# The last two rows of w2 in a decode block: two one-row transfers, the last of them cut into 112, 8 and 8 partitions

## The chip, the cores and the metric

The kernel runs on one core of a Trainium2 chip. The metric is the device time of one execution in microseconds (us), as the median over runs. A profile is one execution of the same program with the hardware profiler on; its span is the time from the first to the last instruction that the profile shows, and its own time is a little longer than that. Times in a profile are counted from the start of the span.

## The reference

One decode step (one token for each of four sequences) of a transformer block: layer norm, attention with grouped heads over the last 2048 entries of a cache, a residual, layer norm, a gated feed-forward part, a residual. All weights are bf16.

```python
def _B_ref(x, w1, w3, w2):            # x: [4, 1, 1024]
    gate = x @ w1                     # w1, w3: [1024, 3584]
    up = x @ w3
    h = silu(gate) * up
    return h @ w2                     # w2: [3584, 1024]

h  = x + A_ref(layernorm(x), k_cache, v_cache, wq, wo)
h2 = h + B_ref(layernorm(h), w1, w3, w2)
```

There are only four tokens, so each weight is read once and used for little arithmetic: 55.58 MB come from memory for about 1.7 thousand small matmuls and weight loads.

## The kernel before

All large inputs (wq, the k and v caches, wo, w1, w3, w2) go through one list, `jobs` (lines 80 to 98). Each job is one transfer of up to 2 MB into a slot of 16 KB for each of 128 partitions; there are ten slots (`NSLOT`, line 18), used in turn. `load_up_to` (line 102) issues jobs in the list's order from SyncE's queue, and `get` (line 115) is called where a job's data are first used: it issues everything up to ten jobs ahead and hands back the view of the slot. Which instruction waits for which is worked out by the tile framework, from the slots and from the semaphores of the transfers: there are eight of these, used in turn by the transfers of SyncE and ScalarE, so a transfer also waits for the one eight places ahead of it.

The order is wq (4 jobs), k (4), v (4), wo (4), w1 (4), w3 (4), w2 (5). In w2, partition p holds the 28 rows from 28p on, of 1024 numbers (2 KB) each. `W2B` (line 94) cuts these 28 rows into jobs of 8, 8, 8, 2 and 2 rows, so the last job brings two rows for each partition, 4 KB in one piece, 512 KB in all.

The product with w2 is at the end of the kernel (lines 365 to 379). For each of a job's rows there are four matmuls (line 371), one for each quarter of the 1024 outputs; they go to four column groups of TensorE and add up in one tile, `y2_ps`, over all 28 rows. The weights that each matmul loads first are the 32 columns of `hg_T` for that row, not w2; w2 is the moving operand. Since a matmul reads all 128 partitions of its row, it needs the whole of that row's transfer. After the last of the 112 matmuls VectorE adds the residual (`res`, line 381), and four stores of 2 KB, two from SyncE and two from ScalarE, write the result (line 384).

Of the kernel before, what the change touches and what calls it, by code (L numbers as in the profile page):

```python
# [10 lines left out]
P = 128  # L11
# [11 lines left out]
def kernel(  # L23
# [19 lines left out]
    nc = tc.nc  # L43
# [36 lines left out]
    jobs = []  # L80
    for i in range(KC // 2):
        jobs.append(("wq", i, [2, NQ], wq_v[:, 2 * i : 2 * i + 2, :]))
    for g in range(Hkv):
        src = A_k_cache[:, g, Sk - W : Sk, :].rearrange("b (p j) d -> p b j d", j=NK)
        jobs.append(("k", g, [B, NK, Dh], src))
    for b in range(B):
        src = A_v_cache[b, :, Sk - W : Sk, :].rearrange("g (p j) d -> p g j d", j=NK)
# [3 lines left out]
    for name, w_v in (("w1", w1_v), ("w3", w3_v)):  # L91
        for i in range(KC // 2):
            jobs.append((name, i, [2, F], w_v[:, 2 * i : 2 * i + 2, :]))
    W2B = [8, 8, 8, 2, 2]
    f0 = 0
    for i, n in enumerate(W2B):
        jobs.append(("w2", i, [n, D], w2_v[:, f0 : f0 + n, :]))
        f0 += n
    place = {(name, i): at for at, (name, i, _, _) in enumerate(jobs)}
    loaded = []  # L100

    def load_up_to(at):
        while len(loaded) < min(at, len(jobs)):
            name, i, shape, src = jobs[len(loaded)]
            slot = stream.tile([P, SLOT], BF16, tag="slot", name="s_" + name)
            n = int(np.prod(shape))
            view = slot[:, :n]
            if len(shape) == 2:
                view = view.rearrange("p (a b) -> p a b", a=shape[0])
            else:  # L110
                view = view.rearrange("p (a b c) -> p a b c", a=shape[0], b=shape[1])
            nc.sync.dma_start(out=view, in_=src)  # L112
            loaded.append(view)

    def get(name, i):
        at = place[(name, i)]
        load_up_to(at + NSLOT)
        return loaded[at]
# [4 lines left out]
    for c in range(C):  # L123
        nc.scalar.dma_start(out=x_nat[R * c : R * c + B, :], in_=x_flat[:, c * DQ : (c + 1) * DQ])
    load_up_to(NSLOT)

    ident = const.tile([P, P], BF16)
# [7 lines left out]
        out=gmask[:, :, 0],  # L135
        in_=ident[:].rearrange("p (b g r) -> p g b r", b=B, g=Hkv),
# [73 lines left out]
    for b in range(B):  # L210
        nc.vector.tensor_copy(
            out=Qm[:, b].rearrange("p (g y) -> p g y", y=QW)[:, :, :REP],
            in_=qT_ps[:, :, :, b].rearrange("p r g -> p g r"),
# [19 lines left out]
    for g in range(Hkv):  # L233
        k = get("k", g)
        for nb in range(NK // JB):
            kT = ktpool.tile([P, B, JB, P], BF16, tag="kT")
            for bb in range(2):
                kt_ps = ps.tile([P, 2, JB, P], BF16, tag=f"kt{n_step % 4}")
                for b2 in range(2):
                    for jj in range(JB):  # L240
                        nc.tensor.transpose(  # L241
                            out=kt_ps[:, b2, jj],
                            in_=k[:, 2 * bb + b2, nb * JB + jj, :],
# [20 lines left out]
        out=Pm[:], in_=sc_ps[:], func=ACT.Exp, bias=nmax[:], scale=qscale, accum_out=rsum[:]  # L264
# [4 lines left out]
    for jb in range(NK // 8):  # L269
        pt_ps = ps.tile([P, 8, P], BF16, tag=f"kt{jb}")  # L270
        for jj in range(8):
            j = jb * 8 + jj
            nc.tensor.transpose(  # L273
                out=pt_ps[:, jj], in_=Pm[:, j * P : (j + 1) * P], identity=ident[:]
# [9 lines left out]
    for j in range(NK):  # L284
# [11 lines left out]
        out=o_sb[:],  # L296
# [69 lines left out]
    fc = 0  # L366
    for i, n in enumerate(W2B):
        w = get("w2", i)
# [46 lines left out]
```

## Time and profile before

| | us |
|---|---|
| median of 3 runs | 141.52 (141.49 to 141.57) |
| the profiled execution | 141.43 |
| its span | 139.4 |
| last transfer of w2 issued, landed | 105.72, 135.45 |
| addition of the residual (line 381) starts | 136.16 |
| first store issued | 136.61 |

How to read it: the chain of waits is followed back from the last instruction, at each step to what released it; 77% of the span lies there in transfers and 16% in TensorE. In the timeline a row gives start, length, engine, line, operation and the number of instructions merged, with the idle time before them in brackets and what ended it. In windows each engine has its busy time and count in a stretch, and the last three numbers are TensorE's granted clock (1.0 is full speed), the mean busy share of the 16 DMA engines, and GB/s. PEld is the loading of weights into TensorE. The trace also holds a record of each DMA packet (start, duration, size and queue, but not which of the 16 engines it ran on) and of each time that a transfer's semaphore rises (its landings, one for each engine that took part).

### The profile page before, as it was taken

The numbers are of one execution on the slowest core, as the hardware profiler recorded it, in microseconds if no ns is written. First come the engines' busy times: TensorE is split into PE (matmuls) and PEld (weight loads), VectorE is DVE, ScalarE is ACT, GpSimd is POOL, SyncE is SP. The second block draws the span as 40 slices with busy tenths as digits, with TensorE's granted clock in tenths as the row PEclk, the third lists the DMA queues.
The fourth block names the chain that finished last, engine by engine and source line by source line (L and its number), as shares of the span: only waits on it lengthen the run. The fifth ranks groups of instructions, "written<-read, shape, count | busy, mean of one in ns | idle before, by whom it ended". The sixth has DMA issues, their size and how long they took to land.

```text
span 139.4 us, 1934 instructions
## 1 busy us (share of the span) xinstructions
PE 69.0 (49%) x848; PEld 42.3 (30%) x848; DVE 32.5 (23%) x58; ACT 26.2 (19%) x27; POOL 2.7 (2%) x10
## 2 busy tenths in 40 slices
PE   0015535499898898039844225272340093352370
PEld 0012111297666574036433213130110041041250
DVE  0023000332443334601110002400019900610001
ACT  1100000135575755266000000310020000000000
POOL 7000000000000000000000000000000000000000
PEclk9999985556999999755896555555555559555555
DMA  5999999999999999999999999999999999999940
GB/s 150 444 414 423 451 437 381 411 425 411 422 424 409 427 420 415 424 413 410 408 404 405 410 441 431 432 424 436 424 432 432 432 432 435 418 437 437 400 197 2
DMA packets 10903, 55.70 MB, mean 400 GB/s; under 512 B 496, under 2 KB 528, under 8 KB 8976
## 3 DMA queue, kind: packets, MB, share of 16 engines
q1 hardware_dynamic: 10848, 55.58, 96.4%
q8 instruction: 6, 0.10, 0.2%
q10 hardware_dynamic: 48, 0.01, 0.0%
q14 instruction: 1, 0.01, 0.0%
HBM read 55.58 MB, written 0.01 MB: 399 GB/s over the span
## 4 chain that ended last, share of the span: by engine, by line
DMA 77%; PE 16%; ACT 2%; SPq 2%; issue 1%; DVE 0%; ACTq 0%
DMA s_w<-in_B_w_dram 41%; DMA s_wo<-in_A_wo_dram 17%; DMA s_k<-in_A_k_cache_dram 14%; PE kt_ps L241 11%; DMA s_wq<-in_A_wq_dram 5%; PE sc_ps L224 3%; ACT kT L249 2%; SPq L112 2%; PE y_ps L319 1%; PE y_ps L371 0%; DVE res L381 0%; ACTq L249 0%
## 5 line engine op out<-in xcount | busy, mean ns | idle before, releaser
L342 PE MATMUL gu_ps<-s_w,n_T 128*32 128x448 bf16 x128 | 12.3, 544 | 18.9 <-DVE eg L357 8.7
L241 PE MATMUL kt_ps<-ident,s_k 128*128 128x128 bf16 x256 | 18.8, 237 | 1.1 <-DMA s_k<-in_A_k_cache_dram 1.1
L249 ACT COPY kT<-kt_ps 128x1024 bf16<-128x1024 bf16 x16 | 15.9, 1013 | 13.4 <-PE kt_ps L241 13.4
L241 PEld LDWEIGHTS <-s_k 128*128 128x128 bf16 x256 | 16.6, 107 | 4.0 <-issue 2.7
L247 DVE COPY kT<-kt_ps 128x1024 bf16<-128x1024 bf16 x16 | 11.1, 692 | 16.2 <-PE kt_ps L241 16.2
L342 PEld LDWEIGHTS <-n_T 128*32 128x32 bf16 x128 | 4.9, 130 | 25.7 <-issue 20.1
L371 PE MATMUL y_ps<-s_w,hg_T 128*32 128x256 bf16 x112 | 6.7, 415 | 9.6 <-DMA s_w<-in_B_w_dram 9.5
L319 PE MATMUL y_ps<-s_wo,oT 128*32 128x256 bf16 x128 | 6.5, 368 | 9.2 <-DMA s_wo<-in_A_wo_dram 8.8
L192 PE MATMUL q_ps<-s_wq,n_T 128*32 128x512 bf16 x64 | 6.6, 567 | 7.6 <-DMA s_wq<-in_A_wq_dram 5.8
L224 PE MATMUL sc_ps<-kT,Qm 128*32 128x512 bf16 x64 | 9.1, 401 | 1.7 <-ACT kT L249 1.4
L371 PEld LDWEIGHTS <-hg_T 128*32 128x32 bf16 x112 | 4.7, 138 | 12.0 <-issue 7.5
L319 PEld LDWEIGHTS <-oT 128*32 128x32 bf16 x128 | 4.7, 124 | 10.7 <-issue 9.6
L147 PE MATMUL sums_ps<-both,ones_f 128*128 128x64 f32 x4 | 1.3, 440 | 11.5 <-DVE both L145 11.5
L157 ACT ACTIVATE rstd<-rstd,eps_t 128x4 f32<-128x4 f32 x2 | 0.6, 297 | 30.7 <-DVE rstd L156 30.7
L286 PE MATMUL o_ps<-s_v,PT 128*32 128x512 bf16 x64 | 5.8, 529 | 0.0
L356 DVE RECIPROCAL eg<-eg 128x896 f32<-128x896 f32 x1 | 5.8, 5753 | 0.0
L192 PEld LDWEIGHTS <-n_T 128*32 128x32 bf16 x64 | 2.4, 126 | 11.0 <-issue 10.7
L273 PE MATMUL pt_ps<-ident,Pm 128*128 128x128 bf16 x16 | 1.9, 312 | 6.0 <-ACT Pm L263 6.0
L147 PEld LDWEIGHTS sums_ps<-both,ones_f 128*128 128x128 f32 x4 | 1.0, 310 | 11.9 <-DVE both L145 9.7
L224 PEld LDWEIGHTS <-Qm 128*32 128x32 bf16 x64 | 2.3, 93 | 6.2 <-issue 5.1
L328 DVE TENSOR_TENSOR h<-y_ps,x_nat 128x256 f32<-128x256 f32 x1 | 0.4, 425 | 15.3 <-PE y_ps L319 15.3
L286 PEld LDWEIGHTS <-PT 128*32 128x32 bf16 x64 | 3.3, 126 | 2.3 <-issue 1.7
(51 smaller groups left out, 32.7 us busy)
## 6 DMA issues: line engine op xcount, KB each, us to landing
s_w<-in_B_w_dram SPq DMA_DIRECT2D x8, 1792.0 KB, 22.2
s_wq<-in_A_wq_dram SPq DMA_DIRECT2D x4, 2048.0 KB, 13.8
s_k<-in_A_k_cache_dram SPq DMA_DIRECT2D x4, 2048.0 KB, 19.5
s_v<-in_A_v_cache_dram SPq DMA_DIRECT2D x4, 2048.0 KB, 23.0
s_wo<-in_A_wo_dram SPq DMA_DIRECT2D x4, 2048.0 KB, 23.3
s_w<-in_B_w_dram SPq DMA_DIRECT2D x3, 2048.0 KB, 35.6
s_w<-in_B_w_dram SPq DMA_DIRECT2D x2, 512.0 KB, 31.3
x_nat<-in_A_x_dram ACTq DMA_DIRECT2D x4, 2.0 KB
```

Of the source, the lines that this page charges most:

```text
L112: nc.sync.dma_start(out=view, in_=src)
L147: nc.tensor.matmul(sums_ps[:], lhsT=ones_f[:], rhs=both[:], start=True, stop=True)
L192: nc.tensor.matmul(q_ps[R * c : R * c + R, hf * HALF : (hf + 1) * HALF, :], lhsT=xn_T[:, kc, :], rhs=w[:, kk, o : o + HALF * Dh], start=(k ...
L224: nc.tensor.matmul(sc_ps[R * b : R * b + R, nb * 512 : (nb + 1) * 512], lhsT=Qm[:, b, g * R : (g + 1) * R], rhs=kT[:, b], start=(g == 0), ...
L241: nc.tensor.transpose(out=kt_ps[:, b2, jj], in_=k[:, 2 * bb + b2, nb * JB + jj, :], identity=ident[:],)
L247: nc.vector.tensor_copy(out=kT[:, 2 * bb : 2 * bb + 2], in_=kt_ps[:])
L249: nc.scalar.copy(out=kT[:, 2 * bb : 2 * bb + 2], in_=kt_ps[:])
L286: nc.tensor.matmul(o_ps[R * b : R * b + R], lhsT=PT[:, j, R * b : R * b + R], rhs=vs[b][:, :, j, :], start=(j == 0), stop=(j == NK - 1), t ...
L319: nc.tensor.matmul(y_ps[R * c : R * c + R, :], lhsT=oT[:, h, :], rhs=w[:, hh, c * DQ : (c + 1) * DQ], start=(h == 0), stop=(h == Hq - 1), ...
L342: nc.tensor.matmul(out_ps[R * c : R * c + R, hf, :FH], lhsT=hn_T[:, kc, :], rhs=w[:, kk, o : o + FH], start=(kc == 0), stop=(kc == KC - 1) ...
L356: nc.vector.reciprocal(out=eg[:], in_=eg[:])
L371: nc.tensor.matmul(y2_ps[R * c : R * c + R, :], lhsT=hg_T[:, fc, :], rhs=w[:, ff, c * DQ : (c + 1) * DQ], start=(fc == 0), stop=(fc == FC ...
```

## The change

`W2B` gets one job more: the last two rows come in two jobs of one row each (2 KB for each partition, 256 KB). The very last job of the list is issued as three transfers, for partitions 0 to 111, 112 to 119 and 120 to 127, all into the same slot. The four matmuls of the last row then need all three. Nothing else is different; the matmuls are the same 112 in the same order.

```diff
-    W2B = [8, 8, 8, 2, 2]
+    W2B = [8, 8, 8, 2, 1, 1]
...
+    def at_end(name, i):
+        return (name, i) == jobs[-1][:2]
...
-            nc.sync.dma_start(out=view, in_=src)
+            if at_end(name, i):
+                for lo, hi in ((0, P - 16), (P - 16, P - 8), (P - 8, P)):
+                    nc.sync.dma_start(out=view[lo:hi], in_=src[lo:hi])
+            else:
+                nc.sync.dma_start(out=view, in_=src)
             loaded.append(view)
```

Line 371, the matmul with w2, becomes line 378; the loads of line 112 become lines 117 and 119.

## The prediction

> **What bounds the kernel now.** I read the page's busy slices first, then the chain of waits, then the end of the timeline, and last short windows of the tail.
>
> ```profile
> PE 69.0 (49%) x848; PEld 42.3 (30%) x848; DVE 32.5 (23%) x58; ACT 26.2 (19%) x27; POOL 2.7 (2%) x10
> DMA  5999999999999999999999999999999999999940
> GB/s 150 444 414 423 451 437 381 411 425 411 422 424 409 427 420 415 424 413 410 408 404 405 410 441 431 432 424 436 424 432 432 432 432 435 418 437 437 400 197 2
> q8 instruction: 6, 0.10, 0.2%
> ```
>
> No engine is busy half the time, and the DMA row stands at 9 from the second slice to the last but two. The kernel is a stream of 55.58 MB at its full rate. What can be changed is what follows the stream, and how evenly its 16 engines finish. The chain of waits shows the end:
>
> ```profile
> 105.72 29.73 DMA s_w<-in_B_w_dram
> 135.45 0.04 issue
> 135.49 0.64 PE y_ps L371 x7
> 136.14 0.02 issue
> 136.16 0.43 DVE res L381
> ```
>
> The last transfer of w2 (two rows of 2 KB for each partition) was issued at 105.72 and landed at 135.45, nearly 30 us later: it lay in the queue behind the others. Then come its eight matmuls, the addition and the stores. Two rows of the timeline and three windows (time, length, engines, granted clock, DMA share, GB/s) show that TensorE is done with all else before then, and how the stream ends:
>
> ```profile
> 133.08 3.04 PE L371 MATMUL y_ps<-s_w,hg_T 128*32 128x256 bf16 x48 [2.96 <-DMA s_w<-in_B_w_dram]
> 135.50 0.14 PEld L371 LDWEIGHTS <-hg_T 128*32 128x32 bf16 x7 [0.40 <-issue]
> 133.50:134.00 0.50, 0.50 (x16) 0.43 (x12) 0.00 (x0) 0.00 (x0) 0.00 (x0) 0.50 0.53 213
> 134.00:134.50 0.50, 0.50 (x16) 0.42 (x12) 0.00 (x0) 0.00 (x0) 0.00 (x0) 0.50 0.42 172
> 134.50:135.00 0.50, 0.50 (x20) 0.41 (x9) 0.00 (x0) 0.00 (x0) 0.00 (x0) 0.50 0.34 139
> ```
>
> From 133.5 on the DMA share is half, then a third. The trace's landing records of the last transfer, one for each engine, say why: nine engines land from 133.70 to 134.12, one at 134.78, six from 135.22 to 135.45 (the slowest three 135.38, 135.41, 135.45). The first transfer landed within 0.45 us (7.57 to 8.02). The six 16 KB packets of the instruction queue (31.2, 43.0, 53.5, 70.4, 91.6, 122.1) each put one more engine about 1.4 us behind; an 8 KB one at 74.4 made the seventh. Every transfer is cut evenly over 16 engines, so this lateness is kept to the end.
>
> **The change, part by part.** The sum is made against the profiled execution: 141.43 us, of which 139.4 are span and 2.0 lie around it. It is 0.09 below the median of the runs shown, 141.52.
>
> (a) *Fewer matmuls after the last landing: four, where there were eight.* In the trace's rows the first four start at 135.49 to 135.50 and take up to 0.40, ending at 135.90; the other four end at 136.11. So 0.21 leaves the path. The same pitch stands in the 48 above: twelve groups of four in 3.04 us, less a gap of 0.3 and the last one's 0.42, are 0.21 each. The four of the row before come when its bytes land, about half a small transfer (0.6 us) earlier, and take that 0.21 while the last row is on its way; without this cover the gain would be gone.
>
> (b) *The wait moves from a matmul to a weight load.* Built, the changed kernel's first weight load of the last row waits for both 8-partition transfers and its matmul for the 112-partition one. Before, the matmul alone waited, with weights loaded ahead. Behind the waiting load stand only this row's seven other instructions and, after them, VectorE's addition. The trace has both kinds for line 342: at 90.33 the load waited and its matmul started 2 ns later, taking 553 ns; at 111.79 the matmul waited and took 532. That is 0.02 and touches only the first of four. A second semaphore may need an instruction of its own: those on TensorE took 0.05, and the next load came 0.08 after its start. Bounds 0.00 and 0.10. I take 0.05, as one of the two waits will usually be over early.
>
> (c) *2 KB pieces in place of 4 KB.* Windows in the stages with 4 KB, 2 KB and 16 KB or 14 KB pieces:
>
> ```profile
> 48.00:60.00 12.00, 6.79 (x88) 4.36 (x83) 5.25 (x7) 6.50 (x7) 0.00 (x0) 0.89 1.02 420
> 64.00:80.00 16.00, 9.16 (x149) 5.92 (x145) 1.04 (x2) 1.85 (x2) 0.00 (x0) 0.71 1.05 407
> 125.00:132.00 7.00, 2.05 (x36) 1.39 (x32) 0.00 (x0) 0.00 (x0) 0.00 (x0) 0.50 1.01 431
> ```
>
> The packet records agree: on one engine a 4 KB packet follows the last after 155.6 ns, a 2 KB one after 80.0. Eight pairs are 8 x (160.0 - 155.6) = 0.035 us more. A further transfer adds one semaphore packet (about 5 ns); three add at most 0.02. I take 0.04 (bounds 0.035 and 0.06).
>
> (d) *The split.* 112 partitions are seven pieces on each of 16 engines. How an 8-partition load is laid out, no row shows; the nearest is the 4-partition load of x, whose semaphore rose once at issue and then four times, one piece on each of four engines. So an 8-partition transfer should take eight engines with one piece each. If both take the same eight, these carry nine pieces in all and the other eight seven, where all had eight: +0.08 for the one half, -0.08 for the other. If they take different halves, 0. The end is set by the slowest of the six late engines, so bounds are -0.08 and +0.08. Were the late engines spread at random over the two halves, the very latest would be in the loaded half one time in two. I take +0.08.
> [...]
>
> (e) *Issue.* SyncE issues three transfers more at 0.33 each (its rows for w2 near the end). It waits for the transfer eight places ahead on its semaphore, so the last small one goes out once w3's last part has landed, at about 118.4. Its turn in the queue comes at about 134, so 15 us hide it. The tenth-last slot, w1's last part, is read long before (by about 102). Only the stores are queued behind on SyncE, and they wait for 136.6. Cost 0; were the cover gone, the stream would stand still for what is late.
>
> Sum: -0.21 + 0.05 + 0.04 + 0.08 = -0.04. The bounds are -0.21 + 0.00 + 0.035 - 0.08 = -0.26 and -0.21 + 0.10 + 0.06 + 0.08 = +0.03. On the profiled execution 141.39, on the median 141.48.
>
> **The rivals.**
>
> *The late engines lie in the spared half.* Then (d) is -0.08, and with a free wait the median comes to 141.26, with (b) as taken 141.32. For it: nothing shows which engines were late. Against it: all of the three latest, which are within 0.07 us, must be in that half, about one time in eight. By itself this stays just within 0.2% (0.28 us, about the least that a measurement of this kernel tells from no change); with 0.03 more from elsewhere it is over.
>
> *The small transfers end one after the other, slower.* If a transfer of eight pieces does not flow behind the one ahead but pays its own way from start to completion, the last landing is late by that. Nearest row: a store of 2 KB at the end is issued at 136.61 and its last landing is recorded at 138.04, so 1.43. One such at the end gives 141.52 + 1.43 - 0.21 + 0.05 + 0.04 = 142.8. It decides from 0.45 us on, where the gain of (a) is eaten and 0.28 passed. Against it: the large transfers follow one another without a gap, 8 x 0.607 = 4.86 for w2's, and their landings are 4.86 apart; the queue is filled 15 us ahead.
> [...]
>
> *The small transfer lies on one engine.* Eight pieces on one are 0.64, two transfers 1.28, less the one piece spared. On one of the nine early engines (at most 134.12) that ends at 135.3 and nothing is seen; on a late one it ends 1.2 later, at about 142.6. The four landings of x speak against it.
>
> *The change does nothing*: if its waits cost all that (a) gains, 141.5, which is inside the forecast.
>
> **How the numbers follow.** Forecast with its own bounds (141.26 to 141.55): 0.75. Late engines spared, and a little more: 0.12. Serial ends: 0.08. One engine: 0.05, half of it unseen. Hence faster by over 0.2%: 0.12. Slower: 0.08 + 0.025, with some for a fetch that falls on an engine already late: 0.12. The rest, 0.76, is within. The range takes the forecast's bounds, and on both sides 0.05 to 0.1 for the spread of the runs (0.08): 141.20 to 141.65; what lies above is left out with about 0.12.
>
> **What would show it.** In the chain, four matmuls instead of eight (0.43 to 0.50 after the landing, not 0.68). In the landing records, the last of the 112-partition transfer and of both small ones, 135.4 to 135.6, and eight landings for each small one. A load of line 378 that starts within 0.1 of the last landing. It is wrong if the last landing comes after 135.8, if the stores' issue moves by more than 0.28, or if a gap opens in the DMA row before 133.5.

## The result, and the profile after

The changed kernel takes 141.88 us (median of 8 runs, 141.67 to 142.06) against 141.52 (8 runs, 141.33 to 141.57): a ratio of 1.0025, 95% interval 1.0016 to 1.0033. It is slower by a quarter of a per cent, outside the range that was forecast. The profiled execution took 141.69, with a span of 139.7. The medians and ratios below leave out one execution that was over 1.5% above the fastest of its kernel, the profiled one of the extra loads into spread partitions.

The end of the chain of waits of the changed kernel (start, length, what):

```profile
105.83 29.86 DMA s_w<-in_B_w_dram
135.70 0.04 issue
135.74 0.80 PE y_ps L378 x7
136.54 0.02 issue
136.56 0.42 DVE res L388
```

The addition starts at 136.56, before the change at 136.16. The chain names the landing of the last row but one (135.70); by the landing records the 112-partition transfer of the last row ends at 136.07, and its four matmuls start 0.04 later. Before, the last landing was at 135.45. So the loss is all ahead of the last landing: that is 0.62 later, while the time from there to the addition fell from 0.71 to 0.49.

Windows of the tail of the changed kernel (time, length, engines with busy time and count, granted clock, DMA share, GB/s):

```profile
133.00:133.50 0.50, 0.25 (x8) 0.21 (x11) 0.00 (x0) 0.00 (x0) 0.00 (x0) 0.50 1.03 406
133.50:134.00 0.50, 0.50 (x16) 0.43 (x12) 0.00 (x0) 0.00 (x0) 0.00 (x0) 0.50 0.74 246
134.00:134.50 0.50, 0.50 (x17) 0.40 (x12) 0.00 (x0) 0.00 (x0) 0.00 (x0) 0.50 0.46 127
134.50:135.00 0.50, 0.50 (x19) 0.32 (x9) 0.00 (x0) 0.00 (x0) 0.00 (x0) 0.50 0.45 172
135.00:135.50 0.50, 0.50 (x12) 0.28 (x8) 0.00 (x0) 0.00 (x0) 0.00 (x0) 0.50 0.28 107
```

Divide GB/s by DMA share, which gives the rate that the busy engines would have if all 16 were busy: 394 and 382 in the first and fourth rows, 332 in the second, 276 in the third. Before the change the rows from 133.5 to 135.0 gave 402, 410 and 409. For about 0.9 us the DMA engines are busy and move less. The packet records show the same piece by piece:

```
packets of queue 1, start in us from the span's start, duration in ns
                       before            after
4 KB, 133.0 to 133.5   159 each          159 each
4 KB, 133.6 to 134.1   159 each          159 to 296, eight of eleven over 159
2 KB, 133.8 to 134.3   (none)            107 to 206, but for one of 84
2 KB, from 134.5       (none)            84, a few to 92
all packets            1 slow after 118  30 slow after 118, 2.2 us in all
```

(Slow means more than 8 ns above the usual duration of its size. One slow packet of 16 KB near 123.1, by 0.5 us, is in both kernels.) The slow 4 KB packets are a clue. They belong to the transfer of rows 24 and 25, which the change does not touch, and by their times they are on the engines that run late: the early ones had landed that transfer by 133.03. They turn slow from 133.57 on, as the early engines come to the pieces of the cut (nine had landed the row before it from 133.29 to 133.75).

### The profile page after: what moved, and what is told of

Same layout as the page of the kernel before. It is cut to its first block, busy times and chain, and to the rows that moved or that the text cites. A ratio compares the mean times of both kernels' runs of the same rounds, so it can differ in the third digit from the quotient of the medians.

```text
span 139.7 us, 1939 instructions
## 1 busy us (share of the span) xinstructions
PE 69.5 (50%) x848; PEld 42.8 (31%) x848; DVE 32.5 (23%) x58; ACT 26.2 (19%) x27; POOL 2.7 (2%) x10
## 4 chain that ended last, share of the span: by engine, by line
DMA 77%; PE 15%; ACT 2%; SPq 2%; issue 1%; DVE 0%; ACTq 0%
DMA s_w<-in_B_w_dram 41%; DMA s_wo<-in_A_wo_dram 17%; DMA s_k<-in_A_k_cache_dram 14%; PE kt_ps L248 11%; DMA s_wq<-in_A_wq_dram 5%; PE sc_ps L231 3%; ACT kT L256 2%; SPq L119 2%; PE y_ps L326 1%; PE y_ps L378 1%; DVE res L388 0%; ACTq L256 0%
## 5 line engine op out<-in xcount | busy, mean ns | idle before, releaser
L326 PE MATMUL y_ps<-s_wo,oT 128*32 128x256 bf16 x128 | 5.9, 345 | 9.7 <-DMA s_wo<-in_A_wo_dram 9.3
L199 PE MATMUL q_ps<-s_wq,n_T 128*32 128x512 bf16 x64 | 7.4, 628 | 6.6 <-DMA s_wq<-in_A_wq_dram 4.8
L378 PEld LDWEIGHTS <-hg_T 128*32 128x32 bf16 x112 | 4.8, 135 | 12.4 <-issue 7.9
L293 PEld LDWEIGHTS <-PT 128*32 128x32 bf16 x64 | 3.9, 127 | 1.7 <-DVE PT L284 0.2
```

The costliest lines, as they stand in the source:

```text
L199: nc.tensor.matmul(q_ps[R * c : R * c + R, hf * HALF : (hf + 1) * HALF, :], lhsT=xn_T[:, kc, :], rhs=w[:, kk, o : o + HALF * Dh], start=(k ...
L293: nc.tensor.matmul(o_ps[R * b : R * b + R], lhsT=PT[:, j, R * b : R * b + R], rhs=vs[b][:, :, j, :], start=(j == 0), stop=(j == NK - 1), t ...
L326: nc.tensor.matmul(y_ps[R * c : R * c + R, :], lhsT=oT[:, h, :], rhs=w[:, hh, c * DQ : (c + 1) * DQ], start=(h == 0), stop=(h == Hq - 1), ...
L378: nc.tensor.matmul(y2_ps[R * c : R * c + R, :], lhsT=hg_T[:, fc, :], rhs=w[:, ff, c * DQ : (c + 1) * DQ], start=(fc == 0), stop=(fc == FC ...
```

## The experiments

Each was timed beside runs of the kernel before on its own chip; the ratios are to those.

**The two one-row jobs without the cut.**

```diff
-    W2B = [8, 8, 8, 2, 2]
+    W2B = [8, 8, 8, 2, 1, 1]
```

> Two jobs of one row (8, 8, 8, 2, 1, 1), each one transfer of 128 partitions, no split. Theory A, the slow packets between 133.6 and 134.5 come from the cut into 112, 8 and 8: no slow packets here, last landing as before plus 0.04, four matmuls less, median 141.30 to 141.42 against 141.52. Theory B, two one-row jobs with 2 KB pieces are what slows the end: 141.75 to 141.95, slow packets stay. Theory C, the slow packets are chance and not the change: a spread of runs like that of the changed kernel, near 141.4 or 141.9 by turns.

Measured 141.34 (11 runs, 141.12 to 141.42), ratio 0.9981 (0.9972 to 0.9989). Windows of its tail:

```profile
133.50:134.00 0.50, 0.50 (x16) 0.43 (x12) 0.00 (x0) 0.00 (x0) 0.00 (x0) 0.50 0.86 340
134.00:134.50 0.50, 0.50 (x16) 0.41 (x12) 0.00 (x0) 0.00 (x0) 0.00 (x0) 0.50 0.49 188
134.50:135.00 0.50, 0.50 (x19) 0.42 (x12) 0.00 (x0) 0.00 (x0) 0.00 (x0) 0.50 0.43 164
```

GB/s over share is 395, 384 and 381: no slow stretch, and no packet over its usual duration in the tail. The last landing, at 135.69, is 2.46 after the last 16 KB part of w2 (133.23); it was 2.41 before the change and is 2.86 with it. The addition starts 0.50 after the last landing, as with the cut. So half of the change gives 0.2% and the cut takes back more than that: theory A stands, B and C fall.

**The cut without the one-row jobs.**

```diff
-    W2B = [8, 8, 8, 2, 1, 1]
+    W2B = [8, 8, 8, 2, 2]
```

(against the changed kernel)

> Jobs as before (8, 8, 8, 2, 2), only the last one cut into 112, 8 and 8 partitions. Theory A, the cut is what costs: slow packets near the end again, now with twice the bytes, median 141.8 to 142.2. Theory B, one-row jobs cost: no slow packets, and the uneven share spares the late engines one piece of 4 KB (0.16), 141.35 to 141.5.

Measured 142.83 (4 runs), ratio 1.0087 (1.0072 to 1.0102), more than the expectation's upper end. The pieces are twice as large, and 97 packets are slow, by 11.0 us in all. Windows:

```profile
133.50:134.00 0.50, 0.50 (x12) 0.44 (x15) 0.00 (x0) 0.00 (x0) 0.00 (x0) 0.50 0.91 238
134.00:134.50 0.50, 0.50 (x20) 0.41 (x12) 0.00 (x0) 0.00 (x0) 0.00 (x0) 0.50 0.77 139
134.50:135.00 0.50, 0.50 (x16) 0.44 (x9) 0.00 (x0) 0.00 (x0) 0.00 (x0) 0.50 0.37 66
```

Here GB/s over share falls to 262, 181 and 178. The loss grows with the bytes in the cut (1.0087 against 1.0025 with half the bytes), not with the number of transfers, which is the same.

**What in the cut costs: the uneven share, or where the pieces go?** Two cuts whose pieces divide evenly by 16 engines, 64 and 64 partitions (four and four for each), and 112 and 16 (seven and one):

```diff
-                for lo, hi in ((0, P - 16), (P - 16, P - 8), (P - 8, P)):
+                for lo, hi in ((0, P // 2), (P // 2, P)):
```

> One-row jobs, the last row cut into 64 and 64 partitions, so all 16 engines have an even share in both. If it is the number of transfers at the end that costs (one more semaphore round each): 141.5 to 141.7, half of what the changed kernel lost against the uncut one. If it is where the pieces are written (a few neighbouring partitions, from many engines at a time): some slow packets, but shorter than in the changed kernel, 141.4 to 141.6. If it is the uneven share alone: as the uncut one-row kernel, 141.3 to 141.45.

Measured 141.74 (12 runs), ratio 1.0016 (1.0006 to 1.0027).

```diff
-                for lo, hi in ((0, P - 16), (P - 16, P - 8), (P - 8, P)):
+                for lo, hi in ((0, P - 16), (P - 16, P)):
```

> One-row jobs, the last row cut into 112 and 16 partitions: even shares on 16 engines (seven pieces and one), but the 16 pieces still go to the same 16 neighbouring partitions. If neighbouring partitions written from many engines at a time are what slows packets: slow packets as in the changed kernel, 141.75 to 142.0. If transfers of only eight engines are what costs: none, 141.3 to 141.5.

Measured 141.85 (11 runs), ratio 1.0021 (1.0011 to 1.0032). Both have slow packets (53 and 34; the profiled execution of 64 and 64, 142.25, was the slowest of its twelve), and both lose what the changed kernel loses or nearly so. The uneven share of the 8-partition transfers is not the cause. 64 and 64 came out above what I expected of the place of writing (141.6 at most), and 0.04 above what I expected of the number of transfers; these two alone do not part the theories. The next does.

**The same number of transfers, each over all 128 partitions.** The last row is cut by columns:

```diff
-                for lo, hi in ((0, P - 16), (P - 16, P - 8), (P - 8, P)):
-                    nc.sync.dma_start(out=view[lo:hi], in_=src[lo:hi])
+                for lo, hi in ((0, D // 2), (D // 2, D)):
+                    nc.sync.dma_start(out=view[:, :, lo:hi], in_=src[:, :, lo:hi])
```

> One-row jobs, the last row cut by columns: two transfers of all 128 partitions with 1 KB each. [...] Theory A1, packets slow down where an engine writes partitions that another engine is writing too: no slow packets, 141.3 to 141.5, as the uncut one-row kernel (141.34). Theory A2, a transfer more at the end costs: 141.6 to 141.8.

Measured 141.28 (11 runs), ratio 0.9981 (0.9972 to 0.9989): the same as uncut, with no slow packet in the tail (each of the 256 packets of 1 KB took 46 ns). Two transfers at the end cost nothing that can be seen; two transfers to half of the partitions each cost 0.35% (0.9981 against 1.0016).

**The same cut in the middle of the stream**, where no engine waits for the end. The first part of w3, 1792 KB or 1.84 MB (written as 1.79 MB in the expectations), is cut into 64 and 64 partitions:

```diff
+    def at_end(name, i):
+        return (name, i) == ("w3", 0)
...
-            nc.sync.dma_start(out=view, in_=src)
+            if at_end(name, i):
+                for lo, hi in ((0, P // 2), (P // 2, P)):
+                    nc.sync.dma_start(out=view[lo:hi], in_=src[lo:hi])
+            else:
+                nc.sync.dma_start(out=view, in_=src)
```

> Jobs as before, and the first part of w3 (1.79 MB, in the middle of the stream) cut into 64 and 64 partitions; bytes, pieces and engine shares are the same. Theory A1: each half is written at a reduced rate while it lasts, half at the worst, so 0.5 to 4.2 us more (142.0 to 145.7), and slow packets in that stretch. Theory A2: one semaphore round more, below 0.1: 141.5 to 141.6.

Measured 147.71 (4 runs), ratio 1.0434 (1.0405 to 1.0463). Its windows:

```profile
104.00:106.00 2.00, 0.79 (x12) 0.00 (x0) 0.21 (x1) 0.92 (x1) 0.00 (x0) 0.50 1.06 229
106.00:108.00 2.00, 0.00 (x0) 0.00 (x0) 1.97 (x2) 0.00 (x0) 0.00 (x0) 0.50 1.01 215
108.00:110.00 2.00, 0.00 (x0) 0.00 (x0) 2.00 (x1) 0.00 (x0) 0.00 (x0) 0.50 1.02 222
114.00:116.00 2.00, 1.41 (x19) 0.47 (x12) 0.00 (x0) 0.00 (x0) 0.00 (x0) 0.50 1.04 444
```

The kernel before, in the same stretch:

```profile
104.00:106.00 2.00, 0.00 (x0) 0.10 (x1) 1.83 (x2) 0.10 (x1) 0.00 (x0) 0.50 1.00 430
106.00:108.00 2.00, 0.00 (x0) 0.00 (x0) 2.00 (x1) 0.00 (x0) 0.00 (x0) 0.50 0.99 423
```

The share is about 1.0 in all of them (a packet counts whole in the window in which it starts, so a share can pass 1): a reader who looks at busy DMA engines alone sees nothing. The rate is half. Two halves of the partitions, issued one after the other, run at 215 to 229 GB/s, where the kernel before has 430 and 423. The loss of 6.1 us is above my upper end of 4.2, which is about what half rate adds for the cut transfer's own bytes. The packet records show the rest. 184 pieces of 14 KB are slow between 99.6 and 111.3, and the cut transfer has only 128, so at least 56 of them belong to uncut transfers beside it. The extra time of all 184, shared over 16 engines, is 5.65 us; the profiled execution lost 5.6 (147.19 against 141.59).

**Is it the writing?** Four loads more that nothing reads, 256 KB each from the same addresses in both kernels, in 16 pieces of 16 KB. Only the partitions written differ:

```diff
+        if name == "w1":
+            for i in range(4):
+                extra = A_k_cache[i, 0, 0:1024, :].rearrange("(p j) d -> p j d", p=16)
+                jobs.append(("xx", i, [64, Dh], extra))
...
+            if name == "xx":
+                nc.sync.dma_start(out=view[112:128], in_=src)
+            else:
+                nc.sync.dma_start(out=view, in_=src)
```

> Jobs as before, and four loads more ahead of w3 that nothing reads: 256 KB each, 16 pieces of 16 KB on 16 engines, all into partitions 112 to 127. Only their bytes counted (1 MB at 430 GB/s) it is 2.4 us more, 144.0. Theory A1 with few places to write through for neighbouring partitions: more than that, up to 9.7 us more if these 16 partitions have a quarter of the rate (151).

Measured 154.01 (4 runs), ratio 1.0866 (1.0843 to 1.0888), 12.4 us above the kernel before (141.59). In the second kernel the partitions are `view[0:128:8]`:

> The same four extra loads from the same addresses, but into partitions 0, 8, 16, ..., 120. If reading from memory or the number of transfers is what slows, it is as with neighbours 112 to 127. Theory A1: less than with neighbours; 2.4 us more at the least, about 4.9 if the 16 partitions reach half of the rate (144.0 to 146.5).

Measured 147.94 (3 runs), ratio 1.0441 (1.0421 to 1.0461), about 6.3 above. Windows of the one with neighbours:

```profile
100.00:102.00 2.00, 0.00 (x0) 0.00 (x0) 0.00 (x0) 0.00 (x0) 0.00 (x0) 0.50 1.04 126
102.00:104.00 2.00, 0.00 (x0) 0.00 (x0) 0.00 (x0) 0.00 (x0) 0.00 (x0) 0.50 1.21 130
104.00:106.00 2.00, 0.05 (x4) 0.05 (x7) 0.00 (x0) 0.00 (x0) 0.00 (x0) 0.50 1.00 107
106.00:108.00 2.00, 1.64 (x16) 0.46 (x15) 0.00 (x0) 0.32 (x1) 0.00 (x0) 0.50 0.94 107
```

and of the one with spread partitions, from an execution that took 149.88:

```profile
100.00:102.00 2.00, 0.00 (x0) 0.00 (x0) 0.00 (x0) 0.00 (x0) 0.00 (x0) 0.50 1.26 205
102.00:104.00 2.00, 0.00 (x0) 0.00 (x0) 0.00 (x0) 0.00 (x0) 0.00 (x0) 0.50 0.85 164
104.00:106.00 2.00, 1.36 (x16) 0.49 (x15) 0.00 (x0) 0.00 (x0) 0.00 (x0) 0.50 1.04 205
```

Same bytes, same addresses read, same number of transfers and pieces, and a DMA share near 1.0 in both (0.94 to 1.21, 0.85 to 1.26): about a quarter of the full rate with neighbours (107 to 130 of 430 GB/s), two fifths to nearly half with spread ones (164 to 205). So what parts the two, 12.4 us against 6.3, is on the writing side: which partitions are written at a time. Why neighbours are slower than spread ones, and spread ones slower than all 128, no run shows. Both totals are above the price of the rates that the expectations supposed, a quarter and half (9.7 and 4.9). With neighbours the packet records show where the time went: 2.4 us for the bytes, 6.0 more in the 64 extra pieces, and 4.5 in 61 slow pieces of the other transfers (each shared over 16 engines), 12.9 together, where the profiled execution (154.60) lost 13.0.

**The change's own cut, in the middle of the stream.** As for 64 and 64, with 112, 8 and 8 partitions:

```diff
-                for lo, hi in ((0, P // 2), (P // 2, P)):
+                for lo, hi in ((0, P - 16), (P - 16, P - 8), (P - 8, P)):
```

> Jobs as before, and the first part of w3 (1.79 MB) cut into 112, 8 and 8 partitions, in the middle of the stream. Theory A1: the two small transfers (115 KB each) fall to 54 to 108 GB/s while they have the stream to themselves, since 16 neighbouring partitions had 108 GB/s; the 112 somewhere between the 215 to 229 of 64 partitions and the full 430. So 2 to 4 us for the small ones, where their bytes are 0.5, and up to 3.5 for the 112: 143 to 147 in all. If the cut's cost was bound to the tail and its late engines: 141.5 to 142.1, the upper end if a loaded engine is a late one (one piece more of 0.53).

Measured 147.96 (5 runs), ratio 1.0443 (1.0425 to 1.0460), above my range of 143 to 147 but far from what the tail alone would give. The rates (the profiled execution took 149.49):

```profile
104.00:106.00 2.00, 0.72 (x8) 0.00 (x0) 0.28 (x1) 0.92 (x1) 0.00 (x0) 0.50 1.08 244
106.00:108.00 2.00, 0.00 (x0) 0.00 (x0) 1.97 (x2) 0.00 (x0) 0.00 (x0) 0.50 1.26 158
108.00:110.00 2.00, 0.00 (x0) 0.00 (x0) 2.00 (x1) 0.00 (x0) 0.00 (x0) 0.50 0.88 122
110.00:112.00 2.00, 0.00 (x0) 0.00 (x0) 2.00 (x1) 0.00 (x0) 0.00 (x0) 0.50 0.87 172
```

Read in the order of issue, both parts of the cut cost: 244 at first, then 122 to 172. What each has of the loss was not measured by itself: a window does not tell one transfer's packets from another's.

**A version with one job fewer.**

```diff
-    W2B = [8, 8, 8, 2, 2]
+    W2B = [8, 8, 8, 3, 1]
```

> Jobs 8, 8, 8, 3, 1, no cut: the last job is one row, as in the uncut one-row kernel, with one job fewer. If the gain there (141.34) is the four matmuls fewer after the last landing (0.21), it is the same here: 141.2 to 141.4. If it is that the last two jobs are each as small as one row, this loses part of it: 141.45.

Measured 141.43 (11 runs), ratio 0.9990 (0.9981 to 0.9998): about half of the gain, but the interval reaches that of the one-row jobs (0.9972 to 0.9989), so a loss against them is not clear. In the profile the 12 matmuls of three rows take 0.64 (three times 0.21) when the next landing follows 0.61 later (135.09 to 135.70). That explains little: the first matmul of the last row starts 0.04 after the landing, as elsewhere, and the addition 0.53 after it, where the uncut one-row kernel has 0.50. The rest stays open. All three versions without a cut by partitions beat both kernels, the uncut one-row jobs and the column cut most clearly, at 0.9981 each.

## Why the prediction was wrong, point by point

- *What bounds the kernel* held: the stream, and how its engines finish. With the change too, one engine after another falls 1.4 us behind and six of them land last.
- *(a), four matmuls less, -0.21.* Right. From the last landing to the addition it is 0.71 before, 0.49 after, 0.50 uncut.
- *(b), the weight load's waits, +0.05.* They cost nothing here: the two small transfers had landed by 135.66, before TensorE came to the waits, and the matmul started 0.04 after the 112-partition transfer. The bounds held.
- *(c), 2 KB pieces, +0.04.* Right within what can be seen: from the last 16 KB part's landing to the last one it is 2.41 before and 2.46 with the uncut rows.
- *(d), the split, +0.08 with bounds of -0.08 and +0.08.* This is the step that failed. It counted pieces and let each take 80 ns wherever it was written; what decided was the partitions written (the column cut has 0.9981, 64 and 64 partitions 1.0016), which the bounds did not hold at all. That both small transfers take the same eight engines, on which the +0.08 rests, no run shows; the trace has eight landings for each, at 134.25 to 135.42 and 134.44 to 135.66. In place of 0.08 at most, the cut costs 0.4 us in the profiled tail (2.86 against 2.46) and 0.44% of the time, about 0.6 us, in the medians (1.0025 against 0.9981); the profiled execution, 141.69, was at the low end of its eight runs. Two of the signs that the prediction named for being wrong came: the last landing after 135.8 (136.07), and the first store 0.40 later (136.61 to 137.01). Its half on engines was right: each small transfer has eight landings for its eight pieces. The coin fell the other way, too: the landings of the small transfers end at 135.42 and 135.66, while the six late engines land their part of the 112 partitions, which was issued ahead of the small ones, at 135.77 to 136.07. Both small ones were thus over on their eight engines before any late one had come to them: if each engine takes its pieces in the order of issue, all six late engines are in the spared half. By the first rival that would have brought 141.26 to 141.32. Instead the time rose.
- *(e), issue, 0.* Right: the last small transfer was issued at 118.52 and its first landing came at 134.44.
- *The rivals.* The serial end is wrong as a mechanism: the latest landings of the 112-partition transfer and the two small ones on their engines come at 135.25, 135.42 and 135.66, not 1.43 apart, and the column cut has as many transfers as 64 and 64 and costs nothing. One engine for a small transfer is wrong by its eight landings. That the late engines lie in the spared half is right if pieces are taken in the order of issue, as argued above, but for the gain it gave a term that the slow packets overran. What the runs point to, the partitions that a transfer writes, was not among them.

How the two go together is in part open. Transfers of all 128 partitions run at 423 to 430 GB/s (the kernel before, 104 to 108), with no slow piece in the tail. In the tail of the changed kernel the early engines take up the cut row while the late ones, on which everything waits, still write 4 KB pieces, and from 133.6 to 134.1 eight of eleven of these take 165 to 296 ns in place of 159. That the late ones' own packets slow down is shown; how the pieces of the cut slow them is not: which engine wrote which partition is not in the records, and whether reading from memory has a part in the cost of the cut was not tested by itself.

Whether giving a late engine's last pieces to others could bring anything was not shown. All four cuts by partitions at the end cost time, 0.16% to 0.87% against the kernel before (64 and 64, and two rows in 112, 8 and 8).

## What to carry to other kernels

Cut a transfer by columns or rows of the matrix, and leave it over all 128 partitions (here the column cut and the uncut rows have 0.9981 each); a cut by partitions can halve the rate of the bytes in it (here 215 to 229 GB/s for 64 and 64 partitions, 423 to 430 uncut), even with the DMA share at 1.0. A busy DMA row does not show this: put GB/s beside it. A smaller last transfer shortens what follows the last landing (here two rows to one: 0.71 to 0.50 us, 0.2% of the time), as long as the work of the one before is done when it lands (argued; three rows and one showed it only faintly).

## What the runs showed of the hardware that was not expected

A quarter of the full rate (107 to 130 of 430 GB/s) for transfers that write 16 neighbouring partitions, with a DMA share of 0.94 to 1.21. Transfers to a part of the partitions, in the middle of the stream, cost more than their own reduced rate: 6.1 where 4.2 was the most by rate, 12.4 where it was 9.7. The rest lies in slow pieces of the uncut transfers that ran at the same time, at least 56 of 184 in the one and 61 in the other.
